# Thirty-two matmuls of ones, written to a tile that nobody reads, at the start of an attention and mixture-of-experts kernel

## The chip, the cores and the metric

The kernel runs on one core of a Trainium2 chip. A core has a matrix engine (TensorE, called PE in the profile, with its weight loads shown apart as PEld), VectorE (DVE), ScalarE (ACT), GpSimd (POOL) and SyncE (SP), which issues most transfers. Each engine works through its own instructions in the order in which the program gives them and waits on semaphores of the others. The metric is the device time of one launch in microseconds (us); lower is better.

## The reference

Eight batches of eight heads of attention over 576 positions, with rotary embedding, and then a mixture of eight experts that takes one expert for each token:

```python
q_rot, k_rot = (rotate(q), rotate(k))
scores = scale * np.matmul(q_rot, k_rot.transpose(0, 1, 3, 2))
scores = scores - np.max(scores, axis=-1, keepdims=True)
attn = np.exp(scores)
attn = attn / (np.sum(attn, axis=-1, keepdims=True) + 1e-09)
out = np.matmul(attn, v)
...
e_idx = np.argmax(x @ w_gate, axis=1)
h = np.maximum(x[mask] @ w1[e], 0.0)
out[mask] = gate_w[mask, None] * eom[mask, e, None] * (h @ w2[e])
```

q, k and v are (8, 8, 576, 64); x is the attention's output as 4608 rows of 512; w1 is (8, 512, 1024) and w2 (8, 1024, 512).

## The kernel before

**Tiling.** Two heads form a pair, so there are 32 pairs. The scores of a pair are cut into nine units: four chunks of 128 queries for each head (line 480), and one unit (the fifth, line 473) that holds the last 64 queries of both heads by a block-diagonal stationary tile `bd`. Query and key are each split into a high and a low part (`kh`, `kl`, and the two planes of `q`), so a unit is six matmuls: kh by q high, kl by q high, kh by q low, each for two halves of 288 keys.

**A unit's way.** `Attention.step(g)` writes unit g in this order: `scores` (PE, line 480 or 473) into one of two PSUM buffers `sc`; `peak` (DVE, line 486), the row maximum `m`; `exp` (ACT, line 495), which reads `sc` and `m` and writes `pm`; then, for the unit before, `turn` (DVE, line 501), a transpose in 32x32 blocks into `pt`. With two buffers the scores of unit g+2 wait until the exponential of unit g has read its buffer.

**The rest of a pair.** A table `EVENTS` gives, by unit, when each further step of a pair is written. The ones that matter here: the rotary embedding of a later pair on POOL (lines 429 and 433, `mult` and `add`), its split into high and low parts (line 403 on ACT, line 411 on POOL); the product with the values, `av0` to `av3`, on PE (line 523), from twelve units behind the pair's first unit on, into a PSUM tile `acc` of four banks; `back` (PE, line 541), which transposes the result; `divide` (DVE, lines 548 to 556). For pair 0 the embedding and the splits run on DVE and ACT (`Pair.start`), and what is left of its queries' low part is written behind unit 0. The units 0 to 11 therefore have only scores on PE; unit 12 is the first that is followed by line 523.

**Afterwards** the tokens are sorted by expert, and PE multiplies with the experts' weights (lines 1070, 1078 and 1120), which come in by transfers through rings of buffers. Nothing in the program goes by a clock: every transfer and every step waits for a buffer or for data.

The order of the instructions on each engine is that of the program's text; no scheduler moves them. `ps_a` is the pool that holds `acc` (one buffer), `px` a pool in SBUF that lives for the whole kernel.

Of the kernel before, what the change touches and what calls it, by code (L numbers as in the profile page):

```python
# [10 lines left out]
F32 = mybir.dt.float32  # L11
F32R = mybir.dt.float32r
BF16 = mybir.dt.bfloat16
# [10 lines left out]
P = 128  # L24
# [44 lines left out]
def list_rows(nb):  # L69
    return -(-nb * S // SLOT) * SLOT  # L70


def slot_counts(nb):


    n0 = min(5, -(-((nb - 2) * S - E * (SLOT - 1)) // SLOT)) if nb > 2 else 0
    n0 = max(0, n0)
    T = nb * S - n0 * SLOT
    n2 = max(0, -(-(T - E * P) // SLOT))
    return n0, n2, (T + E * (P - 1)) // P - 2 * n2  # L80
# [31 lines left out]
class Small:  # L112


    def __init__(self, p):
        self.p, self.tag = p, "sc"
# [9 lines left out]
def body(ctx, tc, nb, offs, qk, v, rope, cst, gates, w, out):  # L126
    nc = tc.nc
    NT = nb * S

    def pool(st, n, b, **k):  # L130
        return st.enter_context(tc.tile_pool(name=n, bufs=b, **k))


    early, main, scores = ExitStack(), ExitStack(), ExitStack()
    cpool = pool(ctx, "cpool", 1, side="left")
    dpool = pool(ctx, "dpool", 1, space=bass.MemoryType.DRAM)
    px, px2 = pool(ctx, "px", 1, side="left"), pool(ctx, "px2", 2, side="left")
    pa2 = pool(main, "pa", 2, side="left")
    pp1, pp2 = pool(early, "pp", 1, side="right"), pool(early, "pp2", 2, side="right")
    ps_a = pool(main, "ps_a", 1, space=PSUM, side="left")  # L140
    ps_s = pool(scores, "ps_s", 2, space=PSUM, side="right")

    small = Small(ps_s)
    pools = px, px2, pa2, pp1, pp2, ps_s, small, ps_a

    xd = dpool.tile([NT, XW], F32, name="xd")

    nl = E * list_rows(nb) // P
    lst = [dpool.tile([nl, P], F32, name=f"lst{c}") for c in range(2)]

    first = Pair.first(tc, pools, qk[0, 0], rope)
    ident = cpool.tile([P, P], F32, name="ident")
    make_identity(nc, ident)
    o = offs[C_TRI]
    ct = cpool.tile([P, o], F32, name="ct")
    cc = lambda i: ct[:, offs[i]:offs[i + 1]]

    stage = pa2.tile([P, 2, S], F32, tag="stage", name="stage", bufs=1).rearrange("p a b -> p (a b)")
    nst = offs[-1] - o
    sc = lambda i: stage[:, offs[i] - o:offs[i + 1] - o]  # L160

    ii = cpool.tile([P, NP, BW], F32, name="ii")
    trib = cpool.tile([P, P], BF16, name="trib")
    oneb = cpool.tile([P, P], BF16, name="oneb")
    cnt = cpool.tile([P, E], F32, name="cnt")

    row = cpool.tile([P, nl], BF16, name="row")
    lists = cpool.tile([P, nl], F32, name="lists")
    zero = stage[:, nst:nst + 256]
    nc.vector.memset(zero, 0.0)  # L170
    nc.scalar.dma_start(out=ct, in_=cst[:, 0:o])
    nc.scalar.dma_start(out=stage[:, 0:nst], in_=cst[:, o:])
    nc.scalar.dma_start(out=ii[:, :, P:].rearrange("p n (h x) -> p n h x", h=2), in_=gates)


    nc.gpsimd.memset(cnt, 0.0)
    nc.gpsimd.memset(lists, 0.0)
    consts = [
        (11, lambda: nc.scalar.copy(ii[:, :, 0:P], ident.unsqueeze(1).broadcast_to((P, NP, P)))),
        (15, lambda: nc.scalar.copy(trib, sc(C_TRI))),  # L180
        (16, lambda: nc.scalar.copy(oneb, sc(C_ONE))),
        (18, lambda: nc.scalar.copy(row, sc(C_ROW))),
    ]

    att = Attention(tc, nb, pools, cc, ident, ii, first, trib, oneb, cnt, zero, qk, v, xd, row, lists)
    n0 = slot_counts(nb)[0]
    moe = Moe(tc, nb, (px, px2, small), cc, ident, cnt, w, xd, lists, lst, out)

    if n0:
        g = att.listed(nb - 3)  # L190
        for k, f in moe.table0():
            att.at(g + k, 2, f)
        att.at(g + 6, 2, moe.fetch)
    att.start(consts)
    for g in range(att.G):
        att.step(g)
    early.close()
    if n0:
        moe.open_right(pool(ctx, "mr", 1, side="right", reuse_waits="tile"))
        moe.begin0()  # L200
    for g in range(att.G, att.G + TURN):
        att.step(g)
    scores.close()
    small.move(pool(ctx, "ps_x", 2, space=PSUM, side="right", reuse_waits="tile"))
    moe.ph = pool(ctx, "ps_h", 1, space=PSUM, side="right", reuse_waits="tile")
    if not n0:
        att.rest(lambda g: True)
        main.close()
        moe.open_right(pool(ctx, "mr", 1, side="right", reuse_waits="tile"))
        left = []  # L210
    else:

        moe.turned_in(0, 0)
        att.rest(lambda g: g <= att.G + 1)
        moe.turned_in(0, 1)
        for h in range(2):
            moe.turn(0, h)
        for u in range(3):
            moe.split(u)
        att.rest(lambda g: g <= att.G + 8)  # L220
        moe.first(0, 0)
        att.rest(lambda g: True)
        main.close()
        moe.first(0, 1)
    moe.open_left(pool(ctx, "ml", 1, side="left", reuse_waits="tile"),
                  pool(ctx, "ps_m", 1, space=PSUM, side="left", reuse_waits="tile"))
    if n0:
        left = att.last + pieces(moe.table1(), 72)
    else:
        for f in att.last + pieces(moe.table1(), 72):  # L230
            f()
        moe.fetch()
        moe.begin0()
        moe.begin1()
    moe.run(left)


def pieces(gen, n):

    return [lambda: next(gen, None) for _ in range(n)]  # L240


class Attention:
# [507 lines left out]
class Moe:  # L751
# [430 lines left out]
    def run(self, left):  # L1182
        left = list(left)
        N = self.end
        self.more(0)
        for s in range(N):
            self.slot(s, left)
        while left:
            left.pop(0)()
        M = len(self.todo)  # L1190
        if N < M:
            rv = self.nc.values_load(self.used[0:1, 0:1], min_val=0, max_val=self.n1,
                                     skip_runtime_bounds_check_because="bounded by the number of tokens")
            with self.tc.If(rv > self.T):
                self.begin0(N, M, "b")
                self.begin1(N)
                self.more(N)
                for s in range(N, M):
                    self.slot(s, [])
# [25 lines left out]
def build(nc, arrays, nb, offs):  # L1225
    args = {n: nc.dram_tensor(f"in_{n}", a.shape, mybir.dt.from_np(a.dtype), kind="ExternalInput").ap() for n, a in arrays.items()}
    out = nc.dram_tensor("out_0", (nb * S, DM), F32, kind="ExternalOutput").ap()
    with tile.TileContext(nc) as tc, tc.manual_schedule(), ExitStack() as ctx:
        body(ctx, tc, nb, offs, args["qk"], args["v"], args["rope"], args["cst"], args["gates"], args["w"], out)
# [14 lines left out]
```

## Time and profile before

| what | us |
|---|---|
| median of 3 runs | 1050.54 |
| lowest and highest of them | 1047.6 and 1051.23 |
| the profiled execution, its own time | 1050.29 |
| span of its trace, first to last instruction | 1048.4 |

PE is busy for 1002.2 us of the span, DVE for 819.4, ACT for 628.6, POOL for 599.5. The span starts at 0; times below are counted from there. The attention ends near 550 us. [...]

### The profile page before, as it was taken

The numbers are of one execution on the slowest core, as the hardware profiler recorded it, in microseconds if no ns is written. First come the engines' busy times: TensorE is split into PE (matmuls) and PEld (weight loads), VectorE is DVE, ScalarE is ACT, GpSimd is POOL, SyncE is SP. The second block draws the span as 40 slices with busy tenths as digits, with TensorE's granted clock in tenths as the row PEclk, the third lists the DMA queues.
The fourth block names the chain that finished last, engine by engine and source line by source line (L and its number), as shares of the span: only waits on it lengthen the run. The fifth ranks groups of instructions, "written<-read, shape, count | busy, mean of one in ns | idle before, by whom it ended". The sixth has DMA issues, their size and how long they took to land.

```text
span 1048.4 us, 34822 instructions
## 1 busy us (share of the span) xinstructions
PE 1002.2 (96%) x14461; PEld 872.3 (83%) x14461; DVE 819.4 (78%) x1371; ACT 628.6 (60%) x1283; POOL 599.5 (57%) x613
## 2 busy tenths in 40 slices
PE   5999999999999999998889999999999999999995
PEld 4888888888888888887778899998889888899984
DVE  6788889898888988888777867667777867857772
ACT  4566666666666666665545444556765765857762
POOL 4777888897988879888740121305343443443621
PEclk9999999999999999999999999999999999999998
DMA  6654665565645657465457966666986977987860
GB/s 217 179 149 131 183 182 140 161 172 172 191 131 173 190 142 205 119 184 135 111 188 280 298 229 194 210 218 234 332 285 221 350 242 270 324 293 253 291 248 28
DMA packets 58209, 216.32 MB, mean 206 GB/s; under 512 B 9351, under 2 KB 9660, under 8 KB 53952
## 3 DMA queue, kind: packets, MB, share of 16 engines
q1 hardware_dynamic: 50304, 194.03, 59.4%
q0 software_dynamic: 6464, 18.92, 5.0%
q8 instruction: 115, 1.88, 0.8%
q10 hardware_dynamic: 1280, 1.11, 0.3%
q14 instruction: 46, 0.38, 0.1%
HBM read 196.04 MB, written 20.09 MB: 206 GB/s over the span
## 4 chain that ended last, share of the span: by engine, by line
PE 66%; DVE 13%; issue 7%; ACT 7%; POOL 5%; DMA 1%; ACTq 0%; POOLq 0%; DVEq 0%
PE py L1120 17%; PE ph L1078 14%; PE sc L480 13%; PE acc L523 11%; ACT pm L495 4%; PE ph L1070 4%; DVE m L486 4%; POOL raw L429 3%; DVE pt L501 2%; DVE wl L1037 2%; PE acc L541 2%; PE mtp L1043 1%; ACT kh L403 1%; ACT wh L1035 1%; DVE xb L548 1%
## 5 line engine op out<-in xcount | busy, mean ns | idle before, releaser
L495 ACT ACTIVATE pm<-sc,m 128x576 f32<-128x576 f32 x288 | 213.3, 741 | 202.7 <-DVE m L486 201.3
L1037 DVE TENSOR_TENSOR wl<-wr,wh 128x1024 fp32r<-128x1024 f32 x184 | 252.6, 1386 | 44.8 <-ACT wh L1035 42.5
L486 DVE TENSOR_REDUCE m<-sc 128x1 f32<-128x576 f32 x288 | 212.8, 739 | 67.0 <-PE sc L480 60.4
L480 PE MATMUL sc<-kh,q 64*128 64x288 f32 x1024 | 222.2, 325 | 20.3 <-ACT q L403 9.9
L501 DVE STREAM_TRANSPOSE pt<-pm 128x576 f32<-128x576 f32 x288 | 219.5, 762 | 0.3 <-ACT pm L495 0.3
L1120 PE MATMUL py<-wh,ht 128*128 128x512 f32 x640 | 215.4, 401 | 0.0
L1035 ACT CAST wh<-wr 128x1024 fp32r<-128x1024 f32 x208 | 212.6, 1050 | 0.0
L523 PE MATMUL acc<-pt,v 32*64 32x128 f32 (+1 forms) x9216 | 198.1, 296 | 9.5 <-issue 4.8
L480 PEld LDWEIGHTS sc<-kh,q 64*128 64x128 f32 x1024 | 147.2, 191 | 62.3 <-ACT pm L495 28.6
L523 PEld LDWEIGHTS acc<-pt,v 32*64 32x64 f32 x9216 | 158.4, 131 | 33.8 <-issue 25.9
L429 POOL TENSOR_TENSOR raw<-raw,rt 128x1152 f32<-128x1152 f32 x62 | 164.1, 2646 | 0.3
L1078 PE MATMUL ph<-xt,wh 128*128 128x256 f32 x896 | 161.1, 282 | 0.5 <-DVE xt L1059 0.5
L1120 PEld LDWEIGHTS py<-wh,ht 128*128 128x128 f32 x640 | 120.2, 188 | 25.7
L1078 PEld LDWEIGHTS ph<-xt,wh 128*128 128x128 f32 x896 | 138.3, 188 | 2.4 <-DVE xt L1059 1.3
L1078 PE MATMUL ph<-xt,wl 128*128 128x256 f32 x448 | 126.1, 281 | 0.0
L1120 PE MATMUL py<-wl,ht 128*128 128x512 f32 x320 | 125.9, 394 | 0.0
L480 PE MATMUL sc<-kl,q 64*128 64x288 f32 x512 | 110.6, 297 | 0.8 <-issue 0.8
L1037 POOL TENSOR_TENSOR wl<-wr,wh 128x1024 fp32r<-128x1024 f32 x24 | 58.4, 2432 | 90.2 <-ACT wh L1035 83.8
L433 POOL TENSOR_TENSOR raw<-raw 128x576 f32<-128x576 f32 x62 | 87.5, 1411 | 1.9
L1094 ACT ACTIVATE ht<-ph 128x512 fp32r<-128x512 f32 x56 | 33.4, 597 | 90.6 <-PE ph L1078 90.6
L480 PEld LDWEIGHTS sc<-kl,q 64*128 64x128 f32 x512 | 84.0, 191 | 1.1 <-issue 1.0
L1078 PEld LDWEIGHTS ph<-xt,wl 128*128 128x128 f32 x448 | 84.4, 188 | 0.1
(247 smaller groups left out, 1304.3 us busy)
## 6 DMA issues: line engine op xcount, KB each, us to landing
wr<-in_w SPq DMA_DIRECT2D x208, 512.0 KB
raw<-in_qk SPq DMA_DIRECT2D x64, 576.0 KB
v<-in_v SPq DMA_DIRECT2D x128, 288.0 KB
xd<-xb SPq DMA_DIRECT2D x16, 513.0 KB
xd<-xb SPq DMA_DIRECT2D x8, 128.2 KB
rt<-in_rope ACTq DMA_DIRECT2D x1, 576.0 KB
xg<-xd,2idx POOLq DMA_INDIRECT x18, 6.2
out<-y,2idx POOLq DMA_INDIRECT x18, 5.6
```

The source lines that it names most:

```text
L429: self.eng(eng).tensor_tensor(out=rv, in0=rv, in1=self.rt[:, 2 * t:2 * t + 2, x], op=ALU.mult)
L433: self.eng(eng).tensor_tensor(out=r[:, 2 * t, x], in0=r[:, 2 * t, x], in1=r[:, 2 * t + 1, x], op=ALU.add)
L480: nc.tensor.matmul(ps[:, a, :HS], self.q[r, w, c * P:c * P + P], mov[r, a * HS:a * HS + HS], start=(n == 0), stop=(n == 2))
L486: nc.vector.tensor_reduce(self.m[i], ps[:, :, :HS], axis=AX.XY, op=ALU.max, negate=True)
L495: nc.scalar.activation(pe.rearrange("p (a b) -> p a b", a=2), self.ps[i][:, :, :HS], AF.Exp, bias=self.m[i], scale=1.0, accum_out=self.z[: ...
L501: self.nc.vector.transpose(out=self.pt[:, st[0] + 5 * st[1] if st else 4, :], in_=self.pc.pop(i))
L523: nc.tensor.matmul(self.acc[h * D:h * D + D, a, o:o + 32 * n], self.v[r, h, j, :], self.pt[r, u:u + n, 32 * j:32 * j + 32], start=(j == 0) ...
L1035: self.nc.scalar.copy(wh, r)
L1037: eng.tensor_tensor(out=wl, in0=r, in1=wh.bitcast(F32), op=ALU.subtract)
L1070: nc.tensor.matmul(ph[:, 0, :], st[:, dc, 0:P], mv[:, dc, :], start=(n == 0), stop=(n == 11))
L1078: nc.tensor.matmul(ph[:, f, :], st[:, dc, fs], mv[:, dc, :], start=(n == 0), stop=(n == 11))
L1120: self.nc.tensor.matmul(py[h], st[:, f, hs], mv, start=(f == 0 and n == 0), stop=(f == 7 and n == 2))
```

## The change

A class `Warm` is added. Its tile `warmx` (128x512, bf16) is filled with ones by a memset on DVE, which comes ahead of the memset of line 170. Its tile `warm` takes the buffer of `acc` in `ps_a` before the first pair does. `run(n)` writes n matmuls on PE, each with the first 128 columns of `warmx` as its stationary operand and all 512 columns as its moving one, into the four banks of `warm` in turn. Nothing reads `warm`. Twenty of them are written ahead of unit 0, and one behind each of the units 0 to 11.

```diff
@@ body
+    warm = Warm(nc, px, ps_a)
     nc.vector.memset(zero, 0.0)
...
     att.start(consts)
+    warm.run(20)
     for g in range(att.G):
         att.step(g)
+        if g < 9 + 3:
+            warm.run(1)
...
+class Warm:
+    def __init__(self, nc, px, ps_a):
+        self.nc = nc
+        self.x = px.tile([P, 512], BF16, name="warmx")
+        nc.vector.memset(self.x, 1.0)
+        self.out = ps_a.tile([P, 4, 512], F32, tag="acc", name="warm")
+        self.n = 0
+
+    def run(self, n):
+        for _ in range(n):
+            self.nc.tensor.matmul(self.out[:, self.n % 4, :], self.x[:, 0:P], self.x, start=True, stop=True)
+            self.n += 1
```

On PE, the program before starts with the units 0, 1 and 2 (`sc_0`, `sc_1`, `sc_2`; `kh`, `kl` and `q` are the split keys and queries):

```order
L480 MATMUL sc_0_163<-kh_150,q_155 128x288 [waits Activation_49]
L480 MATMUL sc_0_163<-kh_150,q_155 128x288
L480 MATMUL sc_0_163<-kl_151,q_155 128x288 [waits DVE_49]
L480 MATMUL sc_0_163<-kl_151,q_155 128x288
L480 MATMUL sc_0_163<-kh_150,q_155 128x288 [waits DVE_49]
L480 MATMUL sc_0_163<-kh_150,q_155 128x288
L480 MATMUL sc_1_180<-kh_150,q_155 128x288 x2
L480 MATMUL sc_1_180<-kl_151,q_155 128x288 x2
L480 MATMUL sc_1_180<-kh_150,q_155 128x288 x2
L480 MATMUL sc_2_195<-kh_150,q_155 128x288 [waits Activation_49]
```

In the changed program the same place, from the last of the twenty on (all line numbers below the new code are 20 higher there):

```order
L259 LDWEIGHTS warmx
L259 MATMUL warm<-warmx 128x512
L500 MATMUL sc_0_186<-kh_153,q_158 128x288 [waits Activation_49]
...
L500 MATMUL sc_0_186<-kh_153,q_158 128x288
L259 LDWEIGHTS warmx
L259 MATMUL warm<-warmx 128x512
L500 MATMUL sc_1_204<-kh_153,q_158 128x288 x2
L500 MATMUL sc_1_204<-kl_154,q_158 128x288 x2
L500 MATMUL sc_1_204<-kh_153,q_158 128x288 x2
L259 LDWEIGHTS warmx
L259 MATMUL warm<-warmx 128x512
L500 MATMUL sc_2_220<-kh_153,q_158 128x288 [waits Activation_49]
```

Each unit's six matmuls and their waits are as they were; a weight load and a matmul of ones stand between one unit and the next.

On DVE, the changed program starts so, up to the first step of the rotary embedding:

```order
L253 MEMSET warmx 128x512
L171 MEMSET stage 128x256
L801 MEMSET fn 128x4
L801 MEMSET fs_123 128x4
L801 MEMSET fs_125 128x4
L449 TENSOR_TENSOR raw_87<-raw_87,rt 128x1152
```

The first row is new; PE's first matmul of ones waits for it, and the other rows stand one place later. The orders of ACT, POOL and SP are unchanged.

## Rows read from the trace of the kernel before

**Rows 1.** Windows of the start and one later stretch; PEclk is the granted clock.
```profile
core 0: us, PE busy (x) PEld busy (x) DVE busy (x) ACT busy (x) POOL busy (x), PEclk, DMA share, GB/s
...
13.88:31.78 17.90, 17.14 (x60) 14.32 (x61) 13.83 (x20) 9.97 (x25) 15.82 (x9) 1.00 0.72 211
...
36.90:60.00 23.10, 22.92 (x548) 19.37 (x555) 19.33 (x32) 14.82 (x39) 16.49 (x12) 1.00 0.41 106
484.15:487.56 3.41, 3.41 (x13) 3.08 (x13) 2.84 (x5) 2.14 (x6) 2.88 (x4) 0.50 0.90 191
```

**Rows 2.** Groups by line and form on PE, 484.2 to 487.1: busy, mean ns.
```profile
L541 PE MATMUL acc<-ii,ac 128*128 128x160 f32 x10 | 3.0, 490 | 0.0
```

**Rows 3.** The same view, 37.6 to 60.
```profile
L480 PE MATMUL sc<-kl,q 64*128 64x288 f32 x24 | 5.0, 290 | 0.0
L541 PE MATMUL acc<-ii,ac 128*128 128x160 f32 x10 | 1.6, 309 | 0.0
```

**Rows 4.** The same view, 13.88 to 31.7.
```profile
L480 PE MATMUL sc<-kl,q 64*128 64x288 f32 x18 | 6.1, 438 | 0.0
```

**Rows 5.** The chain, in order of time: start, duration, what.
```profile
31.78 1.80 PE sc L480 x6
33.58 2.90 PE acc L523 x61
...
37.73 0.99 PE sc L480 x6
38.72 1.57 PE acc L523 x61
```

**Rows 6.** Timeline of units 8 and 10 (start, duration, instruction).
```profile
24.62 0.50 PEld L480 LDWEIGHTS sc<-kh,q 64*128 64x128 f32 x2 [0.38 <-ACT pm L495]
...
26.46 0.76 DVE L486 TENSOR_REDUCE m<-sc 128x1 f32<-128x576 f32 x1 [0.40 <-PE sc L480]
...
28.20 0.50 PEld L480 LDWEIGHTS sc<-kh,q 64*128 64x128 f32 x2 [0.38 <-ACT pm L495]
```

**Rows 7.** Timeline of one unit and the next use of its buffer, 55.84 to 58.67.
```profile
55.84 0.53 PE L480 MATMUL sc<-kh,q 64*128 64x288 f32 x2
...
56.94 0.76 DVE L486 TENSOR_REDUCE m<-sc 128x1 f32<-128x576 f32 x1 [0.96 <-PE sc L480]
...
57.61 0.77 DVE L501 STREAM_TRANSPOSE pt<-pm 128x576 f32<-128x576 f32 x1
...
58.30 0.72 DVE L486 TENSOR_REDUCE m<-sc 128x1 f32<-128x576 f32 x1
...
58.67 0.53 PE L480 MATMUL sc<-kh,q 64*128 64x288 f32 x2
```

**Rows 8.** Timeline of the first 14 us, all engines.
```profile
0.88 0.27 DVE L170 MEMSET stage<- 128x256 f32 x1 [0.88 <-PEq L1240]
...
6.72 1.36 DVE L429 TENSOR_TENSOR raw<-raw,rt 128x1152 f32<-128x1152 f32 x1 [5.54 <-DMA rt<-in_rope]
...
9.92 0.84 PE L480 MATMUL sc<-kh,q 64*128 64x288 f32 x2 [9.92 <-ACT q L403]
...
12.15 0.75 DVE L486 TENSOR_REDUCE m<-sc 128x1 f32<-128x576 f32 x1
...
13.88 0.84 PE L480 MATMUL sc<-kh,q 64*128 64x288 f32 x2 [1.44 <-ACT pm L495]
```

**Rows 9.** Timeline of POOL: the split of the queries of pairs 1 and 2.
```profile
21.94 1.42 POOL L411 TENSOR_TENSOR kl<-raw,kh 128x576 fp32r<-128x576 f32 x1
25.20 1.41 POOL L411 TENSOR_TENSOR q<-raw,q 128x576 fp32r<-128x576 f32 x1 [1.85 <-ACT q L403]
...
41.42 1.41 POOL L411 TENSOR_TENSOR q<-raw,q 128x576 fp32r<-128x576 f32 x1 [4.08 <-ACT q L403]
```

**Rows 10.** Groups by line and form on PE, 600 to 1000.
```profile
L1120 PE MATMUL py<-wl,ht 128*128 128x512 f32 x264 | 103.9, 394 | 0.0
```

**Rows 11.** Timeline of PE ahead of the fall of the clock at 484.15.
```profile
482.78 0.53 PE L480 MATMUL sc<-kh,q 64*128 64x288 f32 x2 [2.33 <-issue]
```

## The prediction

> **What bounds the kernel now.** I read the windows first, then the groups by form, then the chain and the timeline of the first units. Behind the first pair PE is the bound: from 36.90 to 60.00 it is busy for 22.92 of 23.10 us [rows 1], and the chain runs mostly through PE there [rows 5]. Ahead of that PE looks just as full (17.14 of 17.90 us from 13.88 to 31.78, [rows 1]), but it is full at half speed. The column of the granted clock does not say so: it reads 1.00 from the start [rows 1]. The durations do. At a place where the column reads 0.50 [rows 1], the ten matmuls of line 541 take 3.0 us, 490 ns each [rows 2]; where it reads 1.00 in the steady part they take 1.6 us, 309 ns each [rows 3]. The score matmuls with 288 moving columns show the same two lengths: 290 ns from 37.6 on [rows 3] and 438 ns from 13.88 to 31.7 [rows 4]. [...] So the record of the clock begins with its first change, and PE ran at the lower of its two levels up to about 36.9, where the shorter duration sets in. Just ahead of this rise PE had, for the first time, no gap: from 31.78 the chain is PE alone, unit 12 and then line 523 [rows 5], while between the earlier units it waited some 0.3 to 0.4 us each time for the exponential [rows 6].
>
> **What half speed costs, unit by unit.** Two PSUM buffers tie unit g+2 to unit g: scores, maximum, exponential, scores again. At the lower level this loop takes 24.62 to 28.20, that is 3.58 us: 1.84 from the first weight load to the maximum and 1.74 from there to the next use of the buffer [rows 6]. At the higher level it takes 55.84 to 58.67, 2.83 us: 1.10 and 1.73 [rows 7]. All of the difference lies in the matmuls. Two units run in the loop at a time, so a unit costs 1.79 against 1.415 us.
>
> **The change, term by term.**
>
> *The memset of ones.* It goes ahead of the memset of 256 columns, 0.27 us [rows 8]. Bounds: 0.27 (half the bytes per element) and 0.54 us (twice the elements). DVE has nothing to do until 6.72, behind 5.54 us of waiting for a transfer [rows 8], so it costs nothing; without that cover it would be 0.5 us at most.
>
> *The twenty matmuls.* PE's first work is at 9.92, when ScalarE has the first queries [rows 8]. The ones can start at about 0.88 + 0.54 = 1.4. [...] Cost: nothing, with at most some tenths of delay to unit 0, which the next point covers.
>
> *Units 0 and 1.* Nothing is won before 13.88. The maximum of unit 0 stands on DVE behind the rotary embedding of the remaining queries, without idle time ahead of it, at 12.15 [rows 8]; unit 2 needs the exponential of unit 0 and starts at 13.88 [rows 8]. Unit 0 on PE may end a microsecond earlier or later than now and 13.88 stays.
>
> *Units 2 to 11.* Ten units from 13.88 to 31.78 at 1.79 us. At the higher level 10 x 1.415 = 14.15 us: unit 12 starts at 28.03, **3.75 us earlier**. DVE must hold that pace: maximum and transpose start 0.67 and 0.69 us apart [rows 7], 1.36 us for a unit, which is just under 1.415. With no overlap of their durations (0.76 + 0.77 = 1.53) the gain would be 10 x 0.26 = 2.6; the starts of rows 7 are nearer, I take 3.75.
>
> *A matmul of ones behind each.* On PE a unit is 0.99 us at the higher level (unit 14, [rows 5]). [...] I take 0. [...]
>
> *Units 12 and 13.* Unit 12, the first block of line 523 and unit 13 take from 31.78 to 37.73, 5.95 us [rows 5]. At the higher level: 0.99 + 1.57 + 0.99 = 3.55 [rows 5]. **2.4 us earlier.** From unit 14 on the kernel before has the same clock.
>
> *What is late next.* POOL prepares pair 1, in a chain that starts behind DVE's last split of pair 0 and so does not move. The split of the key's low part starts at 21.94 without a wait and takes 1.42; that of the queries follows at 25.20 only because ScalarE's copy is late by 1.85 us [rows 9]. With that wait gone it ends at about 21.94 + 1.42 + 1.41 = 24.8. Unit 9 would start at 13.88 + 7 x 1.415, about 23.8, and its last two matmuls near 24.5, so it waits about **0.3 us**, which goes off. The same split for pair 2 waited 4.08 us for ScalarE [rows 9], so POOL has room there, and everything later waits on buffers or data and moves along.
>
> *Sum.* 3.75 + 2.4 - 0.3 = 5.85 us. The profiled execution took 1050.29 us, so 1044.4; the median of the runs is 0.25 higher. I predict **1044.6**.
>
> [...]
>
> **The rivals.**
>
> *The clock falls between the units and comes back.* With faster matmuls PE idles more: units 0 and 1 are through by about 12.3, and until 13.88 only a matmul of ones or so is left. At 482.78 PE had waited 2.33 us [rows 11], and at 484.15 the clock fell, for 3.41 us [rows 1]. For it: a gap of 1.5 us at the start, and another ahead of 9.92. Against it: the longest is shorter than 2.33 us unless the twenty end before 7.6, and from 13.88 on the ones fill most of what is left. [...]
>
> [...]
>
> *The change does not reach the end.* Something that I hold to move along does not (a transfer, POOL), or the clock would have been up sooner anyway in executions other than the profiled one. Up to all of the gain goes: 1047.5 to 1050.5.
>
> **How the numbers follow.** Forecast 0.62; falls and returns 0.18; gain lost 0.12; slower 0.08. Each fall of the clock later in the kernel, of which there are two and which may come or stay away in another execution, is worth about 1.4 us (3.0 against 1.6, [rows 2, 3]). Range: below, both stay away, 1044.6 - 2.8, about 1042; above, one early fall more, a later one more and a part of the third case, 1049. What a measurement of this kernel can tell from no change is about 0.3%, 3.15 us, so faster means below 1047.4. Forecast and most of the first rival lie there: 0.78. Same: the rest of it and most of the third, 0.15. Slower: 0.07.
>
> **What would show it.** In the changed trace the score matmuls of units 0 to 11 take about 290 ns and not 438; unit 12 starts near 28.3 and the second block of line 523 (now 38.72) near 32.9; from there the rows repeat with a constant shift of nearly 6 us up to the end. The prediction is wrong if durations of 438 ns appear beyond 10 us, if maximum and transpose become 1.53 us a unit, or if the shift shrinks between 40 us and the end.

## The result: slower, and for the most part far from where the ones stand

In twenty executions of each kernel the median goes from 1052.05 to 1061.97 us. The ratio is 1.0068, 95% interval [1.0046, 1.0089]. All ratios here leave out executions more than 1.5% above the fastest of their kernel (four of the changed kernel, three of the run "held, filled to 96" below, one of them at 1543 us), so this one is smaller than the ratio of the medians, 1.0094. The prediction, 1044.6 in a range of 1042 to 1049, was wrong in size and in sign. The executions of the changed kernel spread over 1050.6 to 1073.8 us, those of the kernel before over 1047.6 to 1058.2. The mean granted clock, on record for each execution, goes with it: 0.988 and 0.989 in the three executions of the changed kernel below 1053 us, 0.964 to 0.982 in the others.

The profiled execution of the changed kernel took 1062.55 us. Its page, busy time and clock line:

```profile
span 1060.7 us, 34886 instructions
PE 1017.4 (96%) x14492; PEld 878.8 (83%) x14493; DVE 819.7 (77%) x1372; ACT 629.1 (59%) x1283; POOL 600.6 (57%) x613
PEclk7799999999999999999989999999999999999998
```

The span is 12.3 us longer, PE is busy 15 us longer, the other engines are as they were. The clock line now begins with two slices of 7. The windows of the start (stretch, length, busy time of PE, PEld, DVE, ACT, POOL with the number of instructions in brackets, then the granted clock as a share of full speed):

```profile
core 0: us, PE busy (x) PEld busy (x) DVE busy (x) ACT busy (x) POOL busy (x), PEclk, DMA share, GB/s
9.90:13.88 3.98, 3.81 (x15) 2.57 (x15) 3.94 (x8) 1.54 (x4) 0.69 (x2) 0.66 0.24 73
...
20.00:28.00 8.00, 8.00 (x26) 5.86 (x27) 5.30 (x8) 4.45 (x10) 4.58 (x5) 0.50 0.29 61
28.00:34.00 6.00, 6.00 (x20) 3.86 (x19) 3.79 (x6) 1.72 (x5) 5.92 (x3) 0.50 0.90 279
```

and PE's timeline there (start, duration, instruction; in square brackets the idle time ahead of it and what ended it):

```profile
1.47 5.88 PE L259 MATMUL warm<-warmx 128*128 128x512 bf16 x20 [1.47 <-DVE warmx L253]
9.47 0.53 PE L500 MATMUL sc<-kh,q 64*128 64x288 f32 x2 [2.12 <-ACT q L423]
...
22.14 0.85 PE L500 MATMUL sc<-kh,q 64*128 64x288 f32 x2
...
23.88 0.61 PE L259 MATMUL warm<-warmx 128*128 128x512 bf16 x1
24.42 0.84 PE L500 MATMUL sc<-kh,q 64*128 64x288 f32 x2
...
37.54 2.97 PE L543 MATMUL acc<-pt,v 32*64 32x160 f32 x80
...
43.05 1.64 PE L543 MATMUL acc<-pt,v 32*64 32x160 f32 x80
```

The twenty ran from 1.47 to 7.35 at no cost, their starts about 427 ns apart up to 4.01 and 216 ns from 4.38 on, and the record of the clock, which now has its first change at 4.33, shows the higher level from there. Then PE waited for 2.12 us, went through unit 0 and its matmul of ones, and at 11.15, just inside unit 1, the clock fell to the lower level, for 30.7 us. A unit with its matmul of ones took 22.14 to 24.42, 2.28 us, in place of 1.79. PE had no gap at all between 20 and 34 (nor from there to 41.87), and the clock stayed at 0.50 until 41.87, behind the first block of line 523 (here line 543). The second block, which stood at 38.72 in the chain of before [rows 5], is at 43.05 in this timeline, **4.3 us later**.

That explains some 4.4 of 12.3 us. I followed the start of each unit's maximum through both traces: the shift is 4.4 us at unit 20, 3.8 at unit 108, 7.0 at unit 132, 8.7 at unit 216 and 11.1 at unit 276, and the last 1.2 come behind the attention. It grows in jumps, at places where PE stands idle and nothing in the profile holds it:

```profile
228.31 0.53 PE L500 MATMUL sc<-kh,q 64*128 64x288 f32 x4 [1.88 <-POOL raw L449]
...
420.18 0.49 PE L543 MATMUL acc<-pt,v 32*64 32x160 f32 x5 [1.59 <-issue]
...
487.73 0.52 PE L543 MATMUL acc<-pt,v 32*64 32x128 f32 x14 [1.77 <-issue]
```

(The first is put down to POOL; the scores there need nothing of the tile it names.) Two shorter ones, 0.82 and 0.81 us, end at 353.68 and 359.07. The kernel before had one gap of the kind, which ends at 482.78 [rows 11], so the third of those shown adds little to the shift. Another gap, of 2.9 to 3.5 us, near 521 in the kernel before, is in every kernel of this study at the same step of the program; it is of another kind, as the counts below show. Behind each of the three shown the clock fell:

```profile
229.61:233.02 3.41, 3.41 (x15) 3.08 (x15) 2.94 (x7) 2.14 (x6) 0.92 (x2) 0.50 0.67 143
420.75:424.17 3.42, 3.42 (x56) 3.14 (x60) 1.84 (x3) 0.83 (x2) 3.42 (x3) 0.50 0.93 281
489.02:492.43 3.41, 3.41 (x72) 2.69 (x68) 3.08 (x5) 1.66 (x4) 3.26 (x6) 0.50 0.83 316
```

What stands at these gaps is a transfer of instructions. The page's list of queues has two that carry instructions alone. The larger one has the same packets and bytes before and after (the other, q14, moves 0.38 MB):

```profile
q8 instruction: 115, 1.88, 0.7%
```

The 115 packets are of 16,384 bytes each, 1.88 MB, for some 29,000 instructions on PE, hence about 250 in a packet, at 65 bytes each, if they are PE's. The runs with 192 or more instructions added, below, have 116. In the stretch ahead of the gap that ended at 420.18 one of them is on its way, among half a megabyte of other transfers (the queues between 417.5 and 420.3):

```profile
q1 hardware_dynamic: 265, 0.51, 55.6%
q8 instruction: 1, 0.02, 2.1%
```

It starts at 417.84, and PE stops at 418.58. The other gaps likewise have such a packet in or just ahead of them (225.83, 485.14; 480.37 in the kernel before). Since a packet comes about every 6 us there, that alone could be chance. Counting PE's instructions (matmuls, weight loads, and the few by which it waits) speaks against chance. Between 14 and 1040 us the fourteen traces of this study have 36 gaps of more than 1 us on PE besides the one near 521. Each stands where 190 to 194 remain when the number of instructions ahead of it is divided by 256, that is, at 64 bytes for each in a packet (8641, 16833 and 19649 in the changed kernel, 19906 in the kernel before), and each ends 2.2 to 3.2 us behind the start of a packet, however long it is. For the gap near 521 the remainder is 151 before and 214 in the changed kernel, and PE goes on 9.9 and 3.9 us behind the last packet: what it waits for the profile does not show. The three gaps above all lie in a block of line 523 or just behind one, where PE goes through 160 instructions in 1.6 us. The change adds 64 instructions to PE, at the very start. If the packets are PE's, that moves every later boundary between them to another step of the program.

### The profile page after: what moved, and what is told of

Same layout as the page of the kernel before. It is cut to its first block, busy times and chain, and to the rows that moved or that the text cites. A ratio compares the mean times of both kernels' runs of the same rounds, so it can differ in the third digit from the quotient of the medians.

```text
span 1060.7 us, 34886 instructions
## 1 busy us (share of the span) xinstructions
PE 1017.4 (96%) x14492; PEld 878.8 (83%) x14493; DVE 819.7 (77%) x1372; ACT 629.1 (59%) x1283; POOL 600.6 (57%) x613
## 3 DMA queue, kind: packets, MB, share of 16 engines
q1 hardware_dynamic: 50304, 194.03, 57.9%
q8 instruction: 115, 1.88, 0.7%
## 4 chain that ended last, share of the span: by engine, by line
PE 64%; DVE 13%; issue 8%; ACT 7%; POOL 6%; DMA 1%; ACTq 0%; POOLq 0%; DVEq 0%
PE py L1140 17%; PE ph L1098 14%; PE sc L500 13%; PE acc L543 11%; ACT pm L515 4%; PE ph L1090 4%; DVE m L506 4%; POOL raw L449 3%; DVE pt L521 3%; DVE wl L1057 2%; PE acc L561 2%; PE mtp L1063 1%; ACT wh L1055 1%; ACT kh L423 1%; POOL q L431 1%
## 5 line engine op out<-in xcount | busy, mean ns | idle before, releaser
L1055 ACT CAST wh<-wr 128x1024 fp32r<-128x1024 f32 x208 | 212.6, 1050 | 0.0
L543 PEld LDWEIGHTS acc<-pt,v 32*64 32x64 f32 x9216 | 160.0, 133 | 36.9 <-issue 29.3
```

Of the source, the lines that this page charges most:

```text
L543: nc.tensor.matmul(self.acc[h * D:h * D + D, a, o:o + 32 * n], self.v[r, h, j, :], self.pt[r, u:u + n, 32 * j:32 * j + 32], start=(j == 0) ...
L1055: self.nc.scalar.copy(wh, r)
```

## The experiments

Theory A: the ones behind the units make the start longer, because the clock does not hold. Theory B: the rest comes from where the boundaries of the instruction packets fall, and hangs on the number of instructions that PE has ahead, not on what they do. The times are medians of 20 executions for the change, of 6 for the run with 54 ones and of 12 for the others; the ratio, with its interval, is to the kernel before on the same chip, whose median was 1050.2 to 1053.0 us; the shifts are those of a unit's maximum in the profiled execution against the profiled execution of before, negative is earlier. In four runs the profiled execution is also the fastest of its twelve (twelve behind only; held, filled to 128; 96 short ahead; held, filled to 96), so their shifts show the good end of the spread and not its middle. The edits are against the changed kernel. `run(n, c)` is `run` with c moving columns in place of 512; a matmul with 64 is called short here.

| run | PE instructions added | us | ratio | shift at unit 13 | 20 | 108 | 216 | 276 |
|---|---|---|---|---|---|---|---|---|
| the change | 64 | 1061.97 | 1.0068 [1.0046, 1.0089] | 4.4 | 4.4 | 3.8 | 8.7 | 11.1 |
| twenty ahead only | 40 | 1056.36 | 1.0047 [1.0023, 1.0071] | 0.0 | 1.9 | 1.2 | 7.4 | 7.1 |
| twelve behind only | 24 | 1056.03 | 1.0030 [1.0007, 1.0053] | -3.2 | 2.9 | 3.3 | 5.0 | 1.9 |
| 32 short ahead | 64 | 1059.02 | 1.0076 [1.0048, 1.0104] | 0.1 | 0.1 | 0.3 | 3.7 | 10.8 |
| 54 ones, clock held | 108 | 1066.45 | 1.0119 [1.0070, 1.0168] | -5.2 | -5.1 | -2.4 | 10.3 | 14.5 |
| 128 short ahead | 256 | 1050.35 | 1.0000 [0.9981, 1.0019] | -0.5 | -0.5 | -0.8 | -1.0 | -2.1 |
| held, filled to 128 | 256 | 1051.64 | 1.0010 [0.9994, 1.0026] | -5.5 | -1.4 | -1.6 | -0.7 | -1.3 |
| held by one, filled to 128 | 256 | 1049.55 | 0.9992 [0.9968, 1.0016] | -6.2 | 1.3 | 1.0 | 1.3 | 2.5 |
| 96 short ahead | 192 | 1047.15 | 0.9969 [0.9953, 0.9986] | -0.1 | -0.1 | -0.6 | -0.3 | -3.2 |
| held, filled to 96 | 192 | 1050.41 | 0.9989 [0.9955, 1.0023] | -5.5 | -4.0 | -4.3 | -4.0 | -7.3 |
| held by one, filled to 96 | 192 | 1048.79 | 0.9983 [0.9958, 1.0008] | -4.9 | 0.0 | -0.3 | -0.1 | -3.0 |
| 112 short ahead | 224 | 1047.62 | 0.9976 [0.9959, 0.9992] | -0.7 | -0.8 | -1.6 | -0.5 | -4.2 |
| the change, filled to 96 | 192 | 1050.29 | 0.9973 [0.9949, 0.9997] | -5.7 | -2.3 | -2.3 | -0.7 | -3.4 |

### The two parts of the change alone

The twenty ahead alone:

```diff
-        if g < 9 + 3:
-            warm.run(1)
```

> Only the twenty matmuls of ones ahead of unit 0 are left; the twelve behind the units are gone. Theory A (the ones behind the units made the start longer, because the clock fell near 11 us and a unit with a matmul of ones then holds PE for 2.28 us against a loop of 1.79): the clock rises in the twenty and falls back near 11 us as in the changed kernel, the units then run at 1.79 us, and unit 13 has its maximum within 0.6 us of where it was before (37.8). Rival R (the twenty ahead are what makes the start longer): unit 13 is 2 us or more late. Theory B (the rest of the loss comes from PE's instruction fetches, which sit elsewhere in the program when instructions are added ahead): 40 more instructions move them too, so the gaps of 1.5 to 3 us behind a fetch come at other places than in both kernels, and the time is some us off before, in either direction; without B the time is that of before, within 1.5 us.

The clock rose at 4.32 and fell at 11.15 as in the changed kernel; the units then ran at their old pace at the lower level, and unit 13 is where it was. So the twenty bring nothing and cost nothing at the start, as theory A has it. Yet the kernel is slower, by jumps of the second kind, here in a block of line 523 (541 in this kernel):

```profile
355.67 0.61 PE L541 MATMUL acc<-pt,v 32*64 32x160 f32 x2 [2.63 <-issue]
```

The twelve behind the units alone:

```diff
-    warm.run(20)
```

> Only the twelve matmuls of ones behind the units 0 to 11 are left; the twenty ahead are gone. Theory A: the clock is low from the start, a unit takes 2.28 us on PE in place of 1.79, and unit 13 has its maximum 4 to 5 us later than before, as in the changed kernel (4.4). Rival R: unit 13 within 1 us of before. If PE without a gap were enough to raise the clock, as the prediction argued, it would rise within the first units and unit 13 would be earlier than before. Theory B: 24 more instructions, other places of the gaps behind fetches than in both kernels.

Theory A failed here. The clock did begin low, and a unit with its ones took 2.28 us, but at 21.68 it rose, and held through the units that followed; unit 13 is 3.2 us early, not 4 to 5 late. In this run the clock rose at the end of 9.7 us without a gap (12.00 to 21.68), in the changed kernel it stayed down through 22.0 us (19.87 to 41.87), with the same ones behind the same units. So whether one matmul of ones per unit raises the clock is not settled by its being there; it differed between the two profiled executions, and I cannot say from these runs what decides it. The gain was then lost in one gap, with a packet of instructions at 37.20 and a fall of the clock from 38.75, while PE still waited:

```profile
39.88 1.88 PE L542 MATMUL acc<-pt,v 32*64 32x128 f32 x40 [3.42 <-issue]
```

### The number of instructions alone

```diff
-    warm.run(20)
+    warm.run(32, 64)
...
-        if g < 9 + 3:
-            warm.run(1)
```

> Thirty-two matmuls with 64 moving columns in place of 512, all of them ahead of unit 0, where PE waits: PE's program is as many instructions longer as in the changed kernel (64), at no cost in the units. Theory B (the instructions' number moves the fetches): start as before, unit 13 within 0.6 us; but from 200 us on the gaps behind fetches stand where the changed kernel has them (near 226, 418 and 486 less 4 us) and the end is 4 to 8 us later than before. Rival C (the later loss hangs on the start's delay or is chance): gaps as before, near 480 and 521, and a time within 2 us of before.

The 32 short ones took 1.9 us while PE had nothing to do. The units 2 to 12 run as before (shift 0.1 at unit 13), and up to unit 108 nothing happens. Then come the gaps of the changed kernel, at the same steps of the program, and the falls behind them (rival C is the expectation's: the later loss hangs on the start's delay or is chance):

```profile
223.94 0.54 PE L498 MATMUL sc<-kh,q 64*128 64x288 f32 x4 [1.34 <-issue]
...
414.64 0.49 PE L541 MATMUL acc<-pt,v 32*64 32x160 f32 x5 [1.06 <-issue]
...
484.47 0.52 PE L541 MATMUL acc<-pt,v 32*64 32x128 f32 x14 [1.69 <-issue]
```

```profile
416.63:426.87 10.24, 10.24 (x152) 8.81 (x139) 6.42 (x12) 4.34 (x12) 7.96 (x7) 0.50 0.63 191
484.89:495.13 10.24, 10.24 (x161) 8.77 (x156) 4.61 (x8) 3.39 (x9) 9.87 (x10) 0.50 0.45 146
```

Even the numbers of matmuls left in the interrupted blocks agree: 5 and 14, as in the changed kernel at 420.18 and 487.73. The gaps themselves are 1 to 2 us; the windows show that the falls cost more, 10.24 us at half clock with PE busy throughout, twice. The first of them and its gap of 1.06 us take the shift from 3.7 at unit 216 to 7.9 at unit 250. With a ratio of 1.0076 this kernel loses as much as the change (1.0068), though none of its ones stands in the way of anything. Theory B holds, rival C falls.

A whole block should then change nothing:

```diff
-    warm.run(20)
+    warm.run(128, 64)
...
-        if g < 9 + 3:
-            warm.run(1)
```

> 128 short matmuls of ones (64 moving columns) ahead of unit 0, none behind the units: PE's program is 256 instructions longer, and PE's instructions come in packets of 16384 bytes, which at 64 bytes each are 256. Theory B (what counts is where in the program the boundaries between fetched blocks fall): they fall where they fell before, so the gaps behind fetches stand near 480 and 521 as before, and the time is that of before within 2 us (1049.5 to 1053.5), though four times as many instructions were added as with the 32 short ones, which cost 8 us. Rival C (every instruction ahead costs later, or the start's activity does): 1059 or more. The 128 take some 59 ns each as the 32 did, 7.6 us, and end ahead of 9.5.

1.0000 with four times the instructions. At the start the 128 did raise the clock, from 5.82 to 9.23, but unit 0 began at 9.34 and ran at the lower level as before. The gap near 480 is back where the kernel before had it, ahead of the same scores [rows 11]; the profile puts it down to ACT here, but PE goes on 2.38 us behind the start of a packet, and in the kernel before 2.40:

```profile
481.43 0.53 PE L498 MATMUL sc<-kh,q 64*128 64x288 f32 x2 [2.05 <-ACT ac L550]
```

Three quarters and seven eighths of a block, the same edit with 96 and with 112:

> 96 short matmuls ahead, 192 instructions, three quarters of a block. Theory B: start as before (unit 13 within 0.6 us), the gaps behind fetches at places that are neither those of before nor those of 64 instructions; a time from 1050 to 1062 that no count of instructions gives. Rival C (more instructions, more loss): above the 1059 of the 32 short ones and below the time of the 128.

> 112 short ones ahead, 224 instructions, half way between the 192 that gained and the 256 that did nothing. Theory B: nothing at the start (unit 13 within 0.6 us of before) and a time by the place of the boundaries alone, from 1046 to 1056; the number cannot be told beforehand, but gaps behind fetches account for the difference. Rival C (a share for every instruction added, or for the activity ahead) would put it at 1048 to 1050, between its neighbours.

With 96 the kernel is faster than before, 0.9969 (1047.15 us, below the 1050 to 1062 that I expected), with 112 0.9976, and in both the step up to -3 or -4 us comes at unit 261, where the gap near 480 is missing. The stretch that held it, in the run with 96:

```profile
470.00:500.00 30.00, 29.23 (x637) 24.33 (x625) 26.37 (x53) 18.59 (x50) 28.46 (x37) 1.00 0.57 149
```

So counts of 24 to 108 instructions lose, 256 does nothing, 192 and 224 gain: no share per instruction fits, a place in the block does. The run with 112 by itself does not tell the two apart, since its 1047.62 lies between its neighbours.

### The clock held

```diff
-    warm.run(20)
+    warm.run(26)
...
-            warm.run(1)
+            warm.run(6 if g == 1 else 2)
```

> More ones: 26 ahead of unit 0, 6 behind unit 1 and 2 behind each other unit up to 11 (54 in all, 108 instructions), to leave no gap in which the clock can fall. If the clock stays at the higher level then, a unit is 0.99 + 2 x 0.27 = 1.5 us on PE, units 2 to 12 take 15 us in place of 17.9 and unit 13 has its maximum about 5 us earlier than before; the score matmuls show 290 ns. If gaps were not the cause and the score matmuls with 64 rows pull the clock down whatever stands between them, the clock falls near 11 to 14 us, a unit takes 1.74 + 2 x 0.5 = 2.7 us and unit 13 is 9 to 10 us late. Theory B adds some us of either sign behind 100 us.

The clock rose at 7.25 and stayed up to 222.29. The units 2 to 11 took 15.1 us in place of 17.9, and unit 13 is 5.2 us early. That is the mechanism of the prediction, seen for the first time:

```profile
13.90:29.00 15.10, 14.77 (x80) 9.43 (x81) 13.78 (x20) 10.00 (x26) 14.50 (x9) 1.00 0.80 234
```

That gain and 14.5 us more are gone by unit 276, in the later gaps (108 instructions), of which the worst comes with the longest fall:

```profile
349.06 1.32 PE L543 MATMUL acc<-pt,v 32*64 32x160 f32 x18 [2.10 <-issue]
```

```profile
348.58:365.65 17.07, 16.59 (x192) 14.07 (x194) 8.40 (x16) 5.53 (x15) 9.60 (x7) 0.50 0.55 150
```

Both together, the held clock and a whole block:

```diff
-    warm.run(20)
+    warm.run(88, 64)
+    warm.run(12)
...
-            warm.run(1)
+            warm.run(6 if g == 1 else 2)
```

> The ones that held the clock (6 behind unit 1, 2 behind each other unit up to 11, 12 long ones just ahead of unit 0), filled up with 88 short ones ahead to 128 matmuls, 256 instructions. Theory A and B together: the clock is up before unit 2 and stays, unit 13 has its maximum 4 to 5.5 us earlier than before (5.2 in the run without the filling), the later gaps are those of before, and the time is 1046 to 1048, ratio about 0.995 to 0.997. Rival: if the later loss hangs on the early rise of the clock and not on the number of instructions, unit 13 is early and the time is still above 1055.

and the same with one matmul of ones behind a unit (`warm.run(99, 64)`, `warm.run(12)`, `6 if g == 1 else 1`):

> As the last, with one matmul of ones behind a unit in place of two (6 still behind unit 1) and 99 short ones in place of 88: again 128 in all. If one is enough to hold the clock once it is up, a unit is some 1.42 to 1.5 us and unit 13 is 5.5 to 6 us early; if not, the clock falls after 14 us, a unit takes 2.28 us and unit 13 is 2 to 4 us late. Time 1045.5 to 1047 in the first case, 1053 to 1055 in the second.

Unit 13 is 5.5 and 6.2 us early. The later gaps are those of before and one of 1.5 and 1.3 us that ends at 544.89 and 549.57, which the 128 short ones alone have too, and still the kernels gain nothing measurable. The early units met a gap of their own, in the second block of line 523 (544 here), first with two behind a unit, then with one:

```profile
36.84 0.79 PE L544 MATMUL acc<-pt,v 32*64 32x160 f32 x28 [2.44 <-issue]
```

```profile
36.58 1.36 PE L544 MATMUL acc<-pt,v 32*64 32x160 f32 x28 [2.87 <-issue]
```

```profile
36.51:46.75 10.24, 10.17 (x175) 8.30 (x174) 4.21 (x6) 2.87 (x8) 7.33 (x7) 0.50 0.35 119
```

A packet of instructions starts at 33.89 and at 33.80 in the two, as PE comes to it. The kernel before reaches the same step 5 to 6 us later, 2.5 us behind the start of its packet at 36.92, and passes without a gap. In the second run the shift goes from -6.2 to +1.3 within seven units. I expected 1046 to 1048 and 1045.5 to 1047; the start and the later gaps were as expected, and what I missed is a gap that only the faster start makes.

With 192 instructions, the count that gained by itself (`warm.run(56, 64)`, `warm.run(12)`, 2 behind a unit; and `warm.run(67, 64)`, `warm.run(12)`, 1 behind a unit):

> The ones that hold the clock (6 behind unit 1, 2 behind each other unit up to 11, 12 long ones ahead), filled up with 56 short ones to 96 matmuls, the 192 instructions that as short ones alone were 0.9969 of before. Both theories together: unit 13 is 4 to 5.5 us early as in the run with 128, and the boundary of the first block no longer falls into the second block of line 523, where that run lost 2.4 us in a gap and more by the fall of the clock behind it; so the shift stays near -5 us up to 475 us and grows where the gap near 480 is missing: 1042 to 1045, ratio 0.991 to 0.995. If the early units make fetches late wherever the boundaries are, a gap of 2 to 3 us appears between 30 and 60 us again and the time is 1047 to 1050.

> As the last with one matmul of ones behind a unit in place of two (6 behind unit 1) and 67 short ones, again 96 in all. Unit 13 is 5.5 to 6.2 us early; without an early gap 1041 to 1044, with one 1047 to 1051.

The gap is there again, one step later:

```profile
36.85 0.53 PE L501 MATMUL sc<-kh,q 64*128 64x288 f32 x4 [1.32 <-issue]
```

```profile
37.80 0.54 PE L501 MATMUL sc<-kh,q 64*128 64x288 f32 x4 [1.72 <-issue]
```

In the first of the two no fall of the clock followed in the profiled execution, and its span of 1040.0 us is the shortest of all. In the second the clock fell at 39.32 for 6.8 us. Over the twelve executions the first ranges from 1042.5 to beyond 1060 us with its median at 1050.4, where the 96 short ones alone stay within 1045.8 to 1050.7. The 1042 to 1045 that I expected without an early gap were met in single executions and missed in the middle, which lies at the upper end of the 1047 to 1050 expected with one.

### The change itself, at another place in the block

```diff
+    warm.run(64, 64)
     warm.run(20)
```

> The change itself (twenty long ones ahead, one behind each of the units 0 to 11) with 64 short ones ahead of the twenty, so that PE's program is 192 instructions longer in place of 64. If the place of the boundaries makes most of the change's loss, it goes: the time is that of before or better in the middle, 1046 to 1053, with the widely spread values of the runs whose clock rises early, against 1062 for the change. If the ones themselves make the loss, it is 1058 or more, as the change was. At the start the ones now reach unit 0 without a gap; if the clock holds, unit 13 is 5 us early, if it falls near 12 us as it did in the changed kernel and stays down, 4 us late, and the time is at the lower or the upper end.

0.9973 in place of 1.0068: the same twenty and twelve matmuls of ones, and 64 short ones more. They change two things, the place of the boundaries and, in the profiled execution, the start. The clock was up at unit 2, fell at 15.44 for 3.41 us, and came back by itself while one matmul of ones stood behind each unit; unit 13 is 5.7 us early. Then came the gap of the faster start, 3.4 us lost between units 13 and 20:

```profile
37.29 0.54 PE L501 MATMUL sc<-kh,q 64*128 64x288 f32 x4 [1.98 <-issue]
```

No run shows what makes one of these packets late and another not. The gaps lie where PE spends its instructions fastest, and some in a stretch of heavy transfers (82.1% on q1 from 224 to 228.3 in the changed kernel, against 57.9% over its span, but 55.6% ahead of the gap that ended at 420.18), and the two were not told apart; making the loads of that stretch smaller or earlier was not tried.

## Why the prediction was wrong, point by point

**What bounds the kernel.** Right: the start ran at the lower level up to 36.9, and the column that reads 1.00 there is only the time ahead of the record's first change. The changed kernel's record, which begins at 4.33, then reads 0.50 for the same units, with a mean of 439 ns for the matmuls that took 438. Wrong is the reading of what came ahead of the rise. The waits of 0.38 us in [rows 6] are those of PEld, the weight loads; PE's own matmuls were busy for 12.43 of 12.58 us from 19.20 to 31.78, so PE was as good as without a gap long before the clock rose.

**The memset and the twenty: right.** No cost: the memset took 0.49 us, within its bounds, and the twenty ended at 7.35, ahead of unit 0 at 9.47. How long a matmul of ones takes, and so that twenty of them fit, no row of the kernel before showed; in the changed kernel it was 427 ns from start to start at the lower level and 216 ns at the higher. But a fall of the clock was held to be unlikely because the longest gap would be shorter than 2.33 us "unless the twenty end before 7.6". They did; since unit 0 came at 9.47 the gap was still only 2.12 us, and the clock fell all the same, at 11.15. The 2.33 us of one row were no bound.

**Units 2 to 11, and 12 and 13: the sizes were right, the condition failed.** The step that failed here is that the clock, once up, holds with one matmul of ones behind a unit. The terms, 3.75 and 2.4 less 0.3, give 5.85. Where it did hold with one (and six behind unit 1), unit 13 was 6.2 us early, of which 0.5 belong to an earlier first transfer: 5.7. The 0 for the ones behind the units is a term that no row of the kernel before showed; in that run units 2 to 11 took 14.55 us with their ones (13.34 to 27.89), where I had 14.15 and 0.3 for POOL's split of the queries. Even that wait is there (held by one, filled to 128, unit 9):

```profile
24.26 0.53 PE L501 MATMUL sc<-kh,q 64*128 64x288 f32 x2 [0.29 <-POOL q L432]
```

In the profiled execution of the changed kernel the ones cost and brought nothing: 2.28 us for a unit with its matmul of ones against 1.79, and 4.4 us late. I gave "slower" 0.08, since I took a stretch without a gap for what raises the clock ("Just ahead of this rise PE had, for the first time, no gap"). That was one observation made into a rule, and a misread one. PE had no gap for 22.0 us, and the clock stayed down. What decides it stays open.

**"Everything later waits on buffers or data and moves along": the step that failed.** It counted semaphores and transfers of data, and not those on the queue of instructions, 115 packets here. The rival that the change does not reach the end named transfers and POOL and stopped at the loss of the gain; it had no price for a loss of its own. The 32 short ones show that this alone is worth 1.0076, as much as the whole change (the intervals are too wide to show the start's 4.4 us beside it), and the same change with 64 more short ones is at 0.9973. By the counts above I take it that PE waits there for its own next instructions, though no view says so; it goes on 2.2 to 3.2 us behind the start of a packet.

**The falls of the clock** I had priced at 1.4 us each, from the two of before. Behind the gaps of the experiments they lasted up to 17 us. For the early fall that the upper end of the range counts no run shows a price; those at the start lasted 30.7 us in the changed kernel and 3.41 us in it filled to 96.

**The chances.** 0.78 for faster rested on one trace whose start I had understood and whose later part I took as given.

## What to carry to other kernels

Adding instructions to an engine that goes through them fast is an edit of its own (64 of them, which nothing waited for, made 1.0076 here): run the same number of idle instructions at the same place as a control before you explain a result by what they do. When a kernel changes by less than one per cent in either direction, look at the traces for idle time of the bottleneck that nothing releases, and for the instruction queue's packets just ahead of it; count the engine's instructions up to each such gap, and see whether the counts leave the same remainder when divided by a packet's (here 190 to 194 of 256). And a cause read off a single rise of the clock is a guess until a run has been made to repeat it.

## What the runs showed of the hardware that was not expected

- A queue that carries instructions alone moved 115 packets of 16 KB (1.88 MB). 256 instructions more on PE at the start left the time at 0.999 to 1.001, while 24 to 108 made it 1.003 to 1.012 and 192 made it 0.997 to 0.999. The 36 gaps of more than 1 us besides the one near 521 all stood at one place in 256 of PE's instructions (remainder 190 to 194).
- Within 5 us of the start of 19 of these 36 gaps (1.1 to 3.4 us long) the granted clock fell to 0.50, for 3.4 to 17 us, although PE was busy for nearly all of it (16.59 of 17.07 us in the longest). Behind the other 17, among them one of 2.05 us that ended at 481.43 with the 128 short ones, it did not.
- PE without a gap did not by itself raise the clock: 14 of 14 us busy between 20 and 34 in the changed kernel at 0.50. In the three runs that began with the long matmuls of ones, back to back, it rose 2.9, 2.9 and 5.8 us behind the first of them (at 4.33, 4.32 and 7.25). It rose on 96 to 128 short ones too, at 5.2 to 6.7, for 3.4 us; with 32 short ones, 1.9 us long, it first rose at 37.75.
- A window's column for the granted clock read 1.00 up to the first change on record (37.0 in the kernel before, 4.33 in the changed one), also where the matmuls of ones stood 427 ns apart and not 216, or those with 288 columns took 438 ns and not 290 [rows 3, 4]. The changed kernel's record, at 0.50, has 438 ns for the latter.
